# Attention scores from 64-partition halves, in units of four heads by two rows

## The chip, the core and the metric

The kernel runs on one core of one Trainium2 chip. A core has TensorE (in the rows: PE for matmuls, PEld for loads of the stationary operand), VectorE (DVE), ScalarE (ACT), GpSimd (POOL) and SyncE (SP), which here issues nearly all DMAs. The metric is the device time of one execution in microseconds (us), as the median of several runs.

## What is computed

Pooled-key attention, then a top-1 mixture of experts, then a gated layer. The change lies in the first part; the sizes are batch 8, 8 heads, 576 rows, head width 64, all float32:

```python
k_p = k.reshape(B, H, Sp, pool, D).mean(axis=3)      # pool 8: 72 pooled rows
v_p = v.reshape(B, H, Sp, pool, D).mean(axis=3)
scores = scale * np.matmul(q, k_p.transpose(0, 1, 3, 2))
scores = scores - np.max(scores, axis=-1, keepdims=True)
attn = np.exp(scores)
attn = attn / (np.sum(attn, axis=-1, keepdims=True) + 1e-09)
return np.matmul(attn, v_p)
...
x = _moe_ref(x=x, **moe_kwargs)      # expert = argmax of x @ w_gate, 4608 tokens
return _moe2_ref(x=x, **moe2_kwargs)
```

## The kernel before

Attention runs over 36 tiles of 128 tokens. The tiles go in four groups (`m`) of nine: four tiles for each of the batches 2m and 2m+1, and one "mix" tile that holds the last 64 rows of both. A normal tile takes one row r of every group of four token rows, for all 8 heads.

A tile n has these steps on TensorE, each in float32:

- `emit_qt`: q is turned so that the head width lies on partitions. Two heads lie side by side on the 128 partitions. For tiles whose q was loaded as four rows per descriptor (`four_rows`, `two_rows`; 30 of the 32 normal tiles) this is eight matmuls against an identity (L382), each filling 64 of the 128 columns; the others and the mix tiles take four true transposes (L387).
- `emit_sc`: four matmuls (L399), one for each pair of heads, with 128 partitions of q and a block-diagonal `kbd` of 2 x 72 columns whose other half is zero. The mix tile (L402) splits its tokens into two halves of 64 columns.
- `emit_pt` turns the exponentials (L423); `emit_av` multiplies by v (L433 for the first six tiles, L441 and L444 after).

DVE makes the row maximum, the subtraction, the reciprocal, the gate logits `lgs` and the product `x`; ACT evacuates PSUM and makes the exponential; `store` writes `x` to DRAM, one tile at a time, from five buffers.

`kbd` of a batch is made from sums over rows: for batches 2 to 7 `sum_k` (POOL) and `prep_k` (four matmuls L325) give the first 64 pooled rows, and `load_end`, `sum_k(GB)`, `prep_k(GB)` and `end_k` the last 8 of six batches at once (L325 with `se`). Batches 0 and 1 go by `load_rows` on 72 partitions, `sum_rows` and `rows_k` (four transposes L299).

The order of work is written by hand. The main loop over n issues pt(n), exp(n+1), qt(n+3), place "a", sc(n+2), place "b", av(n), store(n-1), places "c", "d", "e"; every engine takes its own instructions in that order. The table `ORDER` puts loads and k/v preparation of later groups at such places (five to a tile; the first number holds for group 1, the second for groups 2 and 3), all loads and stores go through the one SP queue in that order, and `E1` does the same for batch 1. Large loads share a pool of 36 tiles (`wtile`).

Of the kernel before, what the change touches and what calls it, by code (L numbers as in the profile page):

```python
# [36 lines left out]
GB = (2, 3, 4, 5, 6, 7)  # L37
# [12 lines left out]

E1 = [3, 26, 9, 7, 10, 19, 20, 31, 24]
# [8 lines left out]
C_ID, C_IE, C_OFF, C_P, C_PK, C_TRI, C_TOK, C_END = 0, 128, 136, 144, 147, 211, 339, 375  # L60


def constants():
    c = np.zeros((128, C_END), np.float32)
    p = np.arange(128)
    c[:, C_ID:C_ID + 128] = np.eye(128)
    c[:, C_TRI:C_TRI + 128] = p[:, None] < p[None, :]
    c[p, C_PK + p // 2] = 1.0 / 64
    c[:, C_IE:C_IE + E] = np.arange(E)
# [12 lines left out]
def fused(ctx: ExitStack, tc: tile.TileContext, q, k, v, moe_w_gate, moe_w1, moe_w2,  # L82
# [106 lines left out]
    x_p = actx.enter_context(tc.tile_pool(name="xo", bufs=5))  # L189
# [3 lines left out]
    kbd = [at4.tile([128, 4, 2, NP], F32, name=f"kbd{i}") for i in range(3)]  # L193
# [18 lines left out]
    def load_q(b, rs=(0, 1, 2, 3)):  # L212
        t = kq["q", b] if ("q", b) in kq else [wtile(F32, f"q{z}") for z in range(2)]
        for r in rs:
            nc.sync.dma_start(
                out=t[r // 2][:, 512 * (r % 2):512 * (r % 2) + 512].rearrange("p (h d) -> p h d", h=H),
                in_=q[b, :, 0:512, :].rearrange("h (p r) d -> r p h d", r=4)[r])
        kq["q", b] = t

    def load_q2(b, j):  # L220

        t = kq["q", b] if ("q", b) in kq else [wtile(F32, f"q{z}") for z in range(2)]
        nc.sync.dma_start(
            out=t[j].rearrange("p (h n) -> p h n", h=H),
            in_=q[b, :, 0:512, :].rearrange("h (p r) d -> p h (r d)", r=4)[:, :, 128 * j:128 * j + 128])
        kq["q", b] = t
        two_rows.add((b, j))

    two_rows, four_rows = set(), set()

    def load_q4(b, j):

        t = kq.setdefault(("q", b), [])
        x = wtile(F32, f"q{j}")
        nc.sync.dma_start(
            out=x.rearrange("p (h n) -> p h n", h=4),
            in_=q[b, 4 * j:4 * j + 4, 0:512, :].rearrange("h (p r) d -> p h (r d)", r=4))
        t.append(x)
        four_rows.add(b)

    def load_mix(m):
        x = kv1.tile([128, DM], F32, tag="mxq", name="mxq")
# [7 lines left out]
    def load_end(h4):  # L250

        t = kq.setdefault(("k", GB), [])
        t.append(wtile(F32, f"ke{h4}"))
        for h in range(4):
            nc.sync.dma_start(
                out=t[h4][0:16 * len(GB), 256 * h:256 * h + 256],
                in_=k[GB[0]:GB[-1] + 1, 4 * h4 + h, 512:576, :].rearrange("b (p r) d -> b p (r d)", r=4))

    def rows_of(b):
        return 128 if isinstance(b, int) else 16 * len(b)  # L260

    def sum_k(b):
        n = rows_of(b)
        o = kv1.tile([128, DM], F32, tag="sk", name="sk") if n == 128 else wtile(F32, "se")[:, 0:DM]
        for h4 in range(2):
            x = kq["k", b][h4].rearrange("p (h r d) -> p h r d", h=4, r=4)[0:n]
            nc.gpsimd.tensor_tensor(out=x[:, :, 0:2], in0=x[:, :, 0:2], in1=x[:, :, 2:4], op=ALU.add)
            nc.gpsimd.tensor_tensor(
                out=o[0:n, 256 * h4:256 * h4 + 256].rearrange("p (h d) -> p h d", h=4),
                in0=x[:, :, 0], in1=x[:, :, 1], op=ALU.add)  # L270
        kq["k", "sum", b] = o

# [29 lines left out]
    def rows_k(b):  # L302
        pp = turn("k", b)
        for z in range(2):
            nc.scalar.activation(out=kbd[b % 3][64 * z:64 * z + 64, :, z], in_=pp[64 * z:64 * z + 64],
                                 func=AF.Copy, scale=1.0 / 64)
# [12 lines left out]

    def prep_k(b):  # L320
        n = rows_of(b)
        s_ = kq["k", "sum", b]
        pp = ps.tile([128, 4, n // 2], F32, tag="pp", name="pk")
        for hp in range(4):
            nc.tensor.matmul(pp[:, hp], lhsT=s_[0:n, hp * 128:hp * 128 + 128], rhs=cc[0:n, C_PK:C_PK + n // 2])  # L325
        if isinstance(b, int):
            kb = kbd[b % 3]
            nc.scalar.copy(out=kb[0:64, :, 0, 0:64], in_=pp[0:64])
            nc.scalar.copy(out=kb[64:128, :, 1, 0:64], in_=pp[64:128])
        else:  # L330
            kt = kv1.tile([128, 4, n // 2], F32, tag="kt", name="kt")
            nc.scalar.copy(out=kt, in_=pp)
            for j, c in enumerate(b):
                ends[c] = kt, j

    def end_k(b):
        kb = kbd[b % 3]
        kt, j = ends[b]
        for z in range(2):
            zs = slice(64 * z, 64 * z + 64)  # L340
            nc.scalar.copy(out=kb[zs, :, z, 64:NP], in_=kt[zs, :, 8 * j:8 * j + 8])
# [25 lines left out]

    def emit_qt(n):
        m, i = tl[n]
        pq = ps.tile([128, 4, 128], F32, tag="pq", name="pq")  # L370
        for hp in range(4):
            if i < 8:
                b = 2 * m + i // 4
                r = i % 4
                if b in four_rows or (b, r // 2) in two_rows:
                    for z in range(2):
                        h = 2 * hp + z
                        if b in four_rows:
                            src = kq["q", b][h // 4][:, 256 * (h % 4) + 64 * r:256 * (h % 4) + 64 * r + 64]
                        else:  # L380
                            src = kq["q", b][r // 2][:, 128 * h + 64 * (r % 2):128 * h + 64 * (r % 2) + 64]
                        nc.tensor.matmul(pq[64 * z:64 * z + 64, hp], lhsT=src, rhs=ident)  # L382
                    continue
                src = kq["q", b][r // 2][:, 512 * (r % 2) + 128 * hp:512 * (r % 2) + 128 * hp + 128]
# [3 lines left out]
        qt = at_p.tile([128, 4, 128], F32, tag="qt", name="qt")  # L388
        nc.scalar.copy(out=qt, in_=pq)
        qts[n] = qt  # L390

    def emit_sc(n):
# [3 lines left out]
        for hp in range(4):  # L396
            o = sc[:, hp // 2, 144 * (hp % 2):144 * (hp % 2) + 144]
            if i < 8:
                nc.tensor.matmul(o, lhsT=qt[:, hp], rhs=kbd[(2 * m + i // 4) % 3][:, hp])  # L399
            else:  # L400
                for z in range(2):
                    nc.tensor.matmul(o[64 * z:64 * z + 64], lhsT=qt[:, hp, 64 * z:64 * z + 64],  # L402
                                     rhs=kbd[(2 * m + z) % 3][:, hp])
# [24 lines left out]
    def emit_av(n, between=None):  # L428
# [3 lines left out]
        for h in range(H) if n in PLAIN else ():  # L432
            nc.tensor.matmul(av[:, h // 4, 73 * (h % 4):73 * (h % 4) + 73], lhsT=sb[0:NP, h // 4, h % 4],  # L433
                             rhs=vau[(2 * m + i // 4) % 2][:, h])
        for g in range(2) if n not in PLAIN else ():

            for c in range(3):
                kw = dict(start=c == 0, stop=c == 2, skip_group_check=True)
                o = av[:, g, 73 * c:73 * c + 146]
                if i < 8:  # L440
                    nc.tensor.matmul(o, lhsT=sb[:, g, c], rhs=vbd[(2 * m + i // 4) % 3][:, g, c], **kw)  # L441
# [8 lines left out]
        xf = x_p.tile([128, XW], F32, tag="x", name="x")  # L450
        lh = sm_p.tile([128, 2, 4, E], F32, tag="lh", name="lh")
        nc.vector.tensor_tensor(out=lh, in0=a4[:, :, :, D + 1:73], in1=rs.to_broadcast([128, 2, 4, E]), op=ALU.mult)
        nc.vector.tensor_reduce(out=lgs[:, n], in_=lh.rearrange("p a h e -> p e (a h)"), axis=AX.X, op=ALU.add)
# [4 lines left out]
        else:  # L458
            ac = a4[:, :, :, 0:D]
        nc.vector.tensor_tensor(out=xf[:, 0:DM].rearrange("p (a h d) -> p a h d", a=2, h=4), in0=ac,  # L460
                                in1=rs.to_broadcast([128, 2, 4, D]), op=ALU.mult)
        done[n] = xf
# [3 lines left out]
    def store(n):  # L466
        xf = done.pop(n)
        nc.scalar.copy(out=xf[:, DM:XW], in_=lgs[:, n])
        m, i = tl[n]
        if i < 8:  # L470
            b = 2 * m + i // 4
            nc.sync.dma_start(
                out=x_d[b * S:b * S + 512, :].rearrange("(p r) d -> p r d", r=4)[:, i % 4], in_=xf)
        else:
            for z in range(2):
                t0 = (2 * m + z) * S + 512
                nc.sync.dma_start(out=x_d[t0:t0 + 64, :], in_=xf[64 * z:64 * z + 64])

    def route_steps(n0, n1):
# [3 lines left out]
        def r1():  # L483
# [7 lines left out]
            cand = sm1.tile([128, n, E], F32, tag="rcd", name="rcd")  # L491
# [191 lines left out]
    for j in range(2):  # L683
        steps[f"q{j}"] = lambda b, j=j: load_q4(b, j)
# [6 lines left out]
    for i, f, x in ((E1[0], sum_rows, ("k", 1, 3, nc.vector)), (E1[1], place_v, (0,)), (E1[2], rows_k, (1,)),  # L691
                    (E1[3], sum_rows, ("v", 1, 2, nc.vector)), (E1[4], sum_rows, ("v", 1, 3, nc.vector)),
# [702 lines left out]
```

## Time and profile before

| | |
|---|---|
| median of 3 runs | 1649.22 us (1646.08 to 1649.38) |
| the profiled execution, its own time | 1658.23 us |
| its span, first to last instruction | 1656.4 us |
| TensorE matmul busy | 1601.1 us, 97% |
| VectorE busy | 845.0 us, 51% |
| ScalarE busy | 500.4 us, 30% |
| GpSimd busy | 262.0 us, 16% |
| mean granted TensorE clock | 0.986 |

The profiled execution lies 9.0 us above the median of the runs; 1.8 us of its time lie outside the span. Busy shares are means over stages: attention fills about the first 235 us, and in it VectorE and GpSimd are far busier than their share of the span tells. A granted clock of 1.00 is 2.4 GHz, 0.50 is 1.2 GHz.

### The profile page before, as it was taken

What the parts mean: (1) busy time and instruction counts of PE and PEld (TensorE: products, weight loads), DVE (VectorE), ACT (ScalarE), POOL (GpSimd) and SP (SyncE); (2) the same over time, 40 slices, a digit from 0 to 9 for tenths busy, and PEclk for the clock granted to TensorE, in tenths of its full rate; (3) what the DMA queues carried; (4) which work ended last, traced back from release to release, by engine and by line L of the source; (5) the groups of instructions that cost most, each with busy time, mean ns of one, the idle gap of its engine ahead of it and who ended that gap; (6) DMA issues with size and microseconds to landing.
All of it is one profiled execution on the core that took longest, in us unless ns stands there. A gap on an engine that the chain in (4) does not pass through costs nothing. (4 is left out here: it accounts for less than half of the span.)

```text
span 1656.4 us, 26527 instructions
## 1 busy us (share of the span) xinstructions
PE 1601.1 (97%) x9323; PEld 1382.9 (83%) x9323; DVE 845.0 (51%) x1796; ACT 500.4 (30%) x1052; POOL 262.0 (16%) x362
## 2 busy tenths in 40 slices
PE   8999989999999989999999999999999999999997
PEld 6888888888888978998888888888888888888886
DVE  7667686687867687324443433333443333443222
ACT  3544543455434354322212212121211212122121
POOL 5766472101110111103000000000000000000000
PEclk9989999999999999999999999999999999999999
DMA  7967776376845563217400100010010001000000
GB/s 199 275 144 190 166 111 199 103 250 230 274 154 195 177 217 131 70 52 259 119 13 20 32 13 26 13 39 13 14 34 15 29 13 33 20 1 26 0 26 13
DMA packets 125371, 161.95 MB, mean 98 GB/s; under 512 B 38544, under 2 KB 83728, under 8 KB 125216
## 3 DMA queue, kind: packets, MB, share of 16 engines
q1 hardware_dynamic: 113440, 124.13, 27.0%
q0 software_dynamic: 11776, 35.91, 6.9%
q8 instruction: 78, 1.28, 0.3%
q14 instruction: 77, 0.63, 0.2%
HBM read 116.92 MB, written 43.08 MB: 97 GB/s over the span
## 5 line engine op out<-in xcount | busy, mean ns | idle before, releaser
L1292 DVE SCALAR_TENSOR_TENSOR th<-th,g 128x512 f32<-128x512 f32 (+1 forms) x120 | 76.1, 634 | 470.6 <-ACT th L1291 470.6
L1288 PE MATMUL g<-xl,rh 128*128 128x512 f32 (+1 forms) x576 | 217.3, 377 | 0.0
L1289 PE MATMUL g<-xh,rl 128*128 128x512 f32 (+1 forms) x576 | 217.3, 377 | 0.0
L1287 PE MATMUL g<-xh,rh 128*128 128x512 f32 (+1 forms) x576 | 217.3, 377 | 0.0
L1291 ACT ACTIVATE th<-g 128x512 f32<-128x512 f32 (+1 forms) x120 | 66.6, 555 | 460.6 <-PE g L1289 460.6
L1318 POOL DMA_INDIRECT out_dram<-o,tk x36 | 34.6, 962 | 815.8 <-ACT o L1317 785.4
L1313 PE MATMUL po<-rl,a 128*128 128x512 f32 x360 | 140.3, 390 | 1.6 <-DMA rl<-scr 1.6
L1312 PE MATMUL po<-rh,a 128*128 128x512 f32 x360 | 140.2, 390 | 0.0
L1314 PE MATMUL po<-rh,a 128*128 128x512 f32 x360 | 140.0, 389 | 0.0
L1287 PEld LDWEIGHTS g<-xh,rh 128*128 128x128 f32 x576 | 108.4, 188 | 20.3
L1288 PEld LDWEIGHTS g<-xl,rh 128*128 128x128 f32 x576 | 108.4, 188 | 20.2
L1289 PEld LDWEIGHTS g<-xh,rl 128*128 128x128 f32 x576 | 108.4, 188 | 19.9
L545 PE MATMUL p<-xh,w1h 128*128 128x256 f32 x672 | 110.2, 286 | 11.2 <-DVE hl L548 8.8
L146 ACT CAST a<-th 128x512 fp32r<-128x512 f32 (+1 forms) x120 | 69.3, 578 | 167.2 <-DVE th L1293 167.2
L147 DVE TENSOR_TENSOR a<-th,a 128x512 fp32r<-128x512 f32 (+1 forms) x120 | 76.7, 639 | 77.2 <-ACT a L146 77.2
L1287 PE MATMUL g<-xh,uh 128*128 128x512 f32 (+1 forms) x288 | 108.7, 378 | 1.7 <-DVE th L1293 1.7
L1288 PE MATMUL g<-xl,uh 128*128 128x512 f32 (+1 forms) x288 | 108.6, 377 | 0.0
L1289 PE MATMUL g<-xh,ul 128*128 128x512 f32 (+1 forms) x288 | 108.6, 377 | 0.0
L545 PE MATMUL p<-xh,w1l 128*128 128x256 f32 x672 | 108.0, 283 | 0.0
L545 PEld LDWEIGHTS p<-xh,w1h 128*128 128x128 f32 x672 | 94.3, 193 | 16.1 <-DVE hl L548 9.6
L545 PE MATMUL p<-xl,w1h 128*128 128x256 f32 x672 | 107.7, 283 | 0.0
L548 DVE SCALAR_TENSOR_TENSOR hl<-p,hh 128x256 fp32r<-128x256 f32 x168 | 70.6, 421 | 64.5 <-ACT hh L547 57.3
(283 smaller groups left out, 3025.5 us busy)
## 6 DMA issues: line engine op xcount, KB each, us to landing
st<-in_moe_w_dram SPq DMA_DIRECT2D x64, 512.0 KB
y_d<-ys SPq DMA_DIRECT2D x39, 257.0 KB
v<-in_v_dram SPq DMA_DIRECT2D x32, 288.0 KB
y<-y_d SPq DMA_DIRECT2D x68, 128.0 KB
x_d<-x SPq DMA_DIRECT2D x32, 260.0 KB
q<-in_q_dram SPq DMA_DIRECT2D x15, 512.0 KB
scr<-uh SPq DMA_DIRECT2D x13, 512.0 KB
scr<-ul SPq DMA_DIRECT2D x13, 512.0 KB
```

The lines of the kernel that those rows point to most:

```text
L146: nc.scalar.copy(out=hi, in_=src)
L147: eng.tensor_tensor(out=lo, in0=src, in1=hi, op=ALU.subtract)
L545: nc.tensor.matmul(a, lhsT=w[d][:, fs], rhs=x[:, d], start=j + d == 0, stop=j == 2 and d == 3)
L548: nc.vector.scalar_tensor_tensor(out=lo, in0=a, scalar=0.0, in1=hi, op0=ALU.max, op1=ALU.subtract)
L1287: nc.tensor.matmul(g[:, j], lhsT=wh[:, sl], rhs=hi[:, d], start=d == 0, stop=False)
L1288: nc.tensor.matmul(g[:, j], lhsT=wh[:, sl], rhs=lo[:, d], start=False, stop=False)
L1289: nc.tensor.matmul(g[:, j], lhsT=wl[:, sl], rhs=hi[:, d], start=False, stop=d == 3)
L1291: nc.scalar.activation(out=th, in_=g[:, 0], func=AF.Tanh, scale=0.5)
L1292: nc.vector.scalar_tensor_tensor(out=th, in0=th, scalar=1.0, in1=g[:, 0], op0=ALU.add, op1=ALU.mult)
L1312: nc.tensor.matmul(po, lhsT=a[:, 0, tsl], rhs=wh[:, sl], start=c == 0, stop=False)
L1313: nc.tensor.matmul(po, lhsT=a[:, 0, tsl], rhs=wl[:, sl], start=False, stop=False)
L1314: nc.tensor.matmul(po, lhsT=a[:, 1, tsl], rhs=wh[:, sl], start=False, stop=c == NC2 - 1)
```

## The change

A normal tile becomes a unit of four heads (g = i % 2) and two rows (2j and 2j+1 of every four). Two rows of one head lie next to each other in the load, so q is turned by four true transposes for every unit, with row 2j on partitions 0 to 63 and row 2j+1 on 64 to 127. The scores are then eight matmuls of 64 partitions by 72 columns, alternating between the lower and the upper half, into two PSUM banks. For that, `kbd` holds every head on both halves: `prep_k` takes seven products of 128 columns and two of 64, and `end_k` takes two products for each batch out of row sums of the ends (`load_ends`, `sum_ends`) in three groups of batches, 0, 1 to 3 and 4 to 7. The mix tile uses q padded with zeros and sixteen products in place of eight. Batches 0 and 1 use the same path as the rest. Two units share an `x` tile and are stored after the second; there are three such tiles. The gate logits of two units are reduced together. The load of batch 3's second q half, and the first loads, move.

```diff
-GB = (2, 3, 4, 5, 6, 7)
+EB = ((0,), (1, 2, 3), (4, 5, 6, 7))
...
-    ("q00", 6, 11), ("q10", 15, 18), ("q01", 25, 28), ("q11", 36, 36)]
+    ("q00", 6, 11), ("q10", 15, 18), ("q01", 20, 28), ("q11", 24, 36)]
...
-    x_p = actx.enter_context(tc.tile_pool(name="xo", bufs=5))
+    x_p = actx.enter_context(tc.tile_pool(name="xo", bufs=3))
...
-    kbd = [at4.tile([128, 4, 2, NP], F32, name=f"kbd{i}") for i in range(3)]
+    kbd = [at4.tile([128, H, NP], F32, name=f"kbd{i}") for i in range(3)]
...
+    def load_q(b, g, j=None):
+        t = kq["q", b] if ("q", b) in kq else kq.setdefault(("q", b), {})
+        if g not in t:
+            t[g] = wtile(F32, f"q{g}")
+        c = slice(0, 256) if j is None else slice(128 * j, 128 * j + 128)
         nc.sync.dma_start(
+            out=t[g].rearrange("p (h n) -> p h n", h=4)[:, :, c],
+            in_=q[b, 4 * g:4 * g + 4, 0:512, :].rearrange("h (p r) d -> p h (r d)", r=4)[:, :, c])
...
+    def load_ends(bs, eng=None):
+        x = wtile(F32, "ke")
+        n = len(bs)
+        for h in range(H):
+            (eng or nc.sync).dma_start(
+                out=x[16 * h:16 * h + 16, 0:256 * n].rearrange("p (b n) -> p b n", b=n),
+                in_=k[bs[0]:bs[-1] + 1, h, 512:576, :].rearrange("b (p r) d -> p b (r d)", r=4))
...
+    def both_k(b):
+        return kbd[b % 3].rearrange("p (h o) s -> p o h s", o=2)
+    def of_k(b, h, z):
+        return kbd[b % 3][64 * z:64 * z + 64, (h - z) % 8]
...
-        for hp in range(4):
-            nc.tensor.matmul(pp[:, hp], lhsT=s_[0:n, hp * 128:hp * 128 + 128], rhs=cc[0:n, C_PK:C_PK + n // 2])
+        pp = ps.tile([128, 2, 4, 64], F32, tag="pp", name="pk")
+        for c in range(8):
+            o = pp[:, c % 2, c // 2]
+            if c < 7:
+                nc.tensor.matmul(o, lhsT=s_[:, 64 * c:64 * c + 128], rhs=PK)
+            else:
+                for z in range(2):
+                    h = (7 + z) % 8
+                    nc.tensor.matmul(o[64 * z:64 * z + 64], lhsT=s_[:, 64 * h:64 * h + 64], rhs=PK)
+        nc.scalar.copy(out=both_k(b)[:, :, :, 0:64], in_=pp)
     def end_k(b):
+        pp = ps.tile([128, H, 8], F32, tag="pp", name="pe_")
         for z in range(2):
+            nc.tensor.matmul(pp[64 * z:64 * z + 64], lhsT=ends[b], rhs=cc[:, C_PK + 8 * z:C_PK + 8 * z + 64])
+        nc.scalar.copy(out=kbd[b % 3][:, :, 64:NP], in_=pp)
...
             if i < 8:
-                        nc.tensor.matmul(pq[64 * z:64 * z + 64, hp], lhsT=src, rhs=ident)
+                j, g = i % 4 // 2, i % 2
+                src = kq["q", 2 * m + i // 4][g][:, 256 * hp + 128 * j:256 * hp + 128 * j + 128]
...
             nc.tensor.transpose(pq[:, hp], src, ident)
...
-                nc.tensor.matmul(o, lhsT=qt[:, hp], rhs=kbd[(2 * m + i // 4) % 3][:, hp])
+        if i < 8:
+            for h in range(4):
                 for z in range(2):
+                    nc.tensor.matmul(sc[:, z, NP * h:NP * h + NP], lhsT=qt[64 * z:64 * z + 64, h],
+                                     rhs=of_k(2 * m + i // 4, 4 * (i % 2) + h, z))
+        else:
+            for h in range(H):
+                for y in range(2):
+                    ys_ = slice(64 * y, 64 * y + 64)
+                    nc.tensor.matmul(sc[ys_, h // 4, NP * (h % 4):NP * (h % 4) + NP],
+                                     lhsT=qt[:, h % 2, h // 2, ys_], rhs=kbd[(2 * m + y) % 3][:, h - h % 2])
...
-    keep_warm(28)
-    load_rows(k, 0, "k")
+    keep_warm(24)
+    load_k(0)
     nc.sync.dma_start(out=cc, in_=cst[:, 0:C_TRI])
-    load_q(0, (0,))
+    load_q(0, 0, 0)
+    load_ends(EB[0], nc.scalar)
     load_rows(v, 0, "v")
...
-    load_q(0, (1,))
-    load_q2(0, 1)
-    load_rows(k, 1, "k")
-    load_q4(1, 0)
-    load_q4(1, 1)
+    load_q(0, 1, 0)
+    load_q(0, 0, 1)
+    load_k(1)
+    load_q(0, 1, 1)
+    load_ends(EB[1])
+    load_q(1, 0)
     load_rows(v, 1, "v")
+    load_q(1, 1)
```

How the instructions stand now, at three places. On PE, a normal tile of group 0 into group 1; `pt` is the turned exponentials, `pq` the turned q, `pvg` a part of v's preparation, `sc` the scores. Before:

```order
L423 MATMUL pt<-cc,pe 96x128 x6
L382 MATMUL pq<-cc,q_453 64x128 x4
L382 MATMUL pq<-cc,q_569 64x128 x4
L347 MATMUL pvg<-wg,vt 72x16 x4
L399 MATMUL sc<-kbd_130,qt 128x144 x4
L441 MATMUL av<-vbd_132,ptsb 128x146 x6
```

and now:

```order
L417 MATMUL pt<-cc,pe 96x128 x6
L372 MATMUL pq<-cc,q_560 128x128 x4
L335 MATMUL pvg<-wg,vt 72x16 x4
L390 MATMUL sc<-kbd_130,qt 128x72 x8
L435 MATMUL av<-vbd_132,ptsb 128x146 x6
```

A unit reads one q tile and not two, its q takes four instructions and not eight, and its scores eight of half the columns.

On PE again, where batch 2's keys are made (`pk`, at tile 4). Before:

```order
L433 MATMUL av<-vau_134,ptsb 128x73 x8
L325 MATMUL pk<-cc,sk 128x64 x4
L325 MATMUL pk<-cc,se 128x48 x4
L423 MATMUL pt<-cc,pe 72x128 x8
L387 MATMUL pq<-cc,mxq 128x128 x4
```

and now:

```order
L427 MATMUL av<-vau_134,ptsb 128x73 x8
L318 MATMUL pk<-cc,sk 128x64 x7
L322 MATMUL pk<-cc,sk 64x64 x2
L417 MATMUL pt<-cc,pe 72x128 x8
L372 MATMUL pq<-cc,mxq 128x128 x4
```

The products of the keys are seven and two in place of four, and the four on the ends of six batches are gone.

On SP, the loads ahead of batch 3 (`q_732` and `q_927` before, `q_639` and `q_699` now, are batch 3's two q halves; `k_728`, `k_730`, now `k_722`, `k_724`, its keys; `k_812` and `v_850` on are batch 4's). Before:

```order
L206 DMA k_728<-in_k_dram 128x4x256
L206 DMA k_730<-in_k_dram 128x4x256
L235 DMA q_732<-in_q_dram 128x4x256
L472 DMA x_d<-x 128x520
L206 DMA k_812<-in_k_dram 128x4x256
L206 DMA k_814<-in_k_dram 128x4x256
L472 DMA x_d<-x 128x520
L278 DMA v_850<-in_v_dram 72x2x512
L278 DMA v_852<-in_v_dram 72x2x512
L278 DMA v_854<-in_v_dram 72x2x512
L278 DMA v_856<-in_v_dram 72x2x512
L235 DMA q_927<-in_q_dram 128x4x256
```

and now:

```order
L216 DMA q_639<-in_q_dram 128x4x256
L481 DMA x_d<-x 128x520 x2
L216 DMA q_699<-in_q_dram 128x4x256
L205 DMA k_722<-in_k_dram 128x4x256
L205 DMA k_724<-in_k_dram 128x4x256
L205 DMA k_808<-in_k_dram 128x4x256
L205 DMA k_810<-in_k_dram 128x4x256
```

Both q halves of batch 3 now stand ahead of its keys, and ahead of batch 4's keys and values.

## Rows read from the trace of the kernel before

**Rows 1.** Windows: stretch, length; busy us (instructions) by engine; granted clock, DMA share, GB/s.

```profile
29.60:85.90 56.30, 51.40 (x513) 47.07 (x513) 39.11 (x84) 28.54 (x70) 41.43 (x52) 1.00 0.90 240
85.90:100.00 14.10, 14.10 (x76) 13.16 (x77) 5.26 (x9) 4.05 (x9) 5.65 (x8) 0.53 0.86 173
100.00:235.00 135.00, 126.44 (x1207) 115.89 (x1206) 103.95 (x274) 70.54 (x177) 87.75 (x117) 0.97 0.68 156
```

**Rows 2.** Timeline of PE: start, length, line, out<-in, [idle before]. Two tiles.

```profile
208.75 0.82 PE L423 MATMUL pt<-cc,pe 128*96 128x128 f32 x6
209.50 1.09 PE L382 MATMUL pq<-cc,q 128*64 128x128 f32 x16
210.52 1.25 PE L399 MATMUL sc<-kbd,qt 128*128 128x144 f32 x8
211.61 1.66 PE L441 MATMUL av<-vbd,ptsb 96*128 96x146 f32 x12
213.11 0.82 PE L423 MATMUL pt<-cc,pe 128*96 128x128 f32 x6
213.76 0.60 PE L387 MATMUL pq<-cc,mxq 128*128 128x128 f32 x4
214.20 1.15 PE L399 MATMUL sc<-kbd,qt 128*128 128x144 f32 x8
```

**Rows 3.** Timeline, a mix tile's product with v, in two column halves.

```profile
131.25 0.13 PEld L444 LDWEIGHTS av<-both,ptsb 96*64 96x64 f32 x1
131.25 0.34 PE L444 MATMUL av<-both,ptsb 96*64 96x146 f32 x1
131.25 0.13 PEld L444 LDWEIGHTS av<-vbd,ptsb 96*64 96x64 f32 x1
131.25 0.34 PE L444 MATMUL av<-vbd,ptsb 96*64 96x146 f32 x1
...
131.42 0.29 PE L444 MATMUL av<-both,ptsb 96*64 96x146 f32 x1
...
131.55 0.29 PE L444 MATMUL av<-both,ptsb 96*64 96x146 f32 x1
```

**Rows 4.** Timeline of PE, products of few moving columns behind full stationary loads.

```profile
31.29 1.90 PE L433 MATMUL av<-vau,ptsb 72*128 72x73 f32 x16
33.03 0.42 PE L299 MATMUL ptk<-cc,sk 72*128 72x72 f32 x4
...
50.97 1.09 PE L325 MATMUL pk<-cc,se 96*128 96x48 f32 x8 [0.83 <-ACT kbd L329]
```

**Rows 5.** Timeline of PE, batch 4's keys, and the product after them.

```profile
148.22 1.00 PE L325 MATMUL pk<-cc,sk 128*128 128x64 f32 x8
149.06 1.71 PE L441 MATMUL av<-vbd,ptsb 96*128 96x146 f32 x12
```

**Rows 6.** Timeline of PE, the waits for loads of q.

```profile
22.50 1.09 PE L382 MATMUL pq<-cc,q 128*64 128x128 f32 x16
...
29.62 0.66 PE L382 MATMUL pq<-cc,q 128*64 128x128 f32 x8 [1.41 <-DMA q<-in_q_dram]
...
34.25 1.09 PE L382 MATMUL pq<-cc,q 128*64 128x128 f32 x16
...
85.88 0.66 PE L382 MATMUL pq<-cc,q 128*64 128x128 f32 x8 [3.03 <-DMA q<-in_q_dram]
...
140.62 0.66 PE L382 MATMUL pq<-cc,q 128*64 128x128 f32 x8 [1.12 <-DMA q<-in_q_dram]
```

**Rows 7.** Timeline of SP, the issue of batch 3's second q half.

```profile
69.19 0.39 SPq L235 DMA_DIRECT2D q<-in_q_dram  x1
```

**Rows 8.** Windows, columns as in Rows 1: the front, and a stretch of group 2.

```profile
0.00:29.62 29.62, 24.31 (x165) 15.34 (x166) 20.38 (x23) 9.34 (x17) 14.42 (x28) 1.00 0.85 220
121.00:138.00 17.00, 16.73 (x176) 15.21 (x175) 13.38 (x33) 8.35 (x22) 13.19 (x20) 1.00 1.01 251
```

More of the change, by code (lines that the diff above doesn't have):

```diff
@@ L248, in load_mix @@
         kq["q", "mix", m] = x
[L250 to L260, printed above, removed]
+    def load_ends(bs, eng=None):
[5 more added lines that the diff above has]
+                in_=k[bs[0]:bs[-1] + 1, h, 512:576, :].rearrange("b (p r) d -> p b (r d)", r=4))
+        kq["ke", bs] = x
@@ new lines, in add_four, with sum_ends @@
+    def add_four(o, x, eng):
+        if eng is nc.vector:
+            eng.tensor_reduce(out=o, in_=x.rearrange("p h r d -> p h d r"), axis=AX.X, op=ALU.add)
+            return
+        eng.tensor_tensor(out=x[:, :, 0:2], in0=x[:, :, 0:2], in1=x[:, :, 2:4], op=ALU.add)
+        eng.tensor_tensor(out=o, in0=x[:, :, 0], in1=x[:, :, 1], op=ALU.add)
+    def sum_ends(bs, eng=None):
+        n = len(bs)
+        o = kv1.tile([128, 256], F32, tag="es", name="es") if n > 1 else kv1.tile([128, D], F32, tag="es0", name="es0")
+        add_four(o[:, 0:64 * n].rearrange("p (b d) -> p b d", b=n),
+                 kq["ke", bs][:, 0:256 * n].rearrange("p (b r d) -> p b r d", b=n, r=4), eng or nc.gpsimd)
+        for j, b in enumerate(bs):
+            ends[b] = o[:, 64 * j:64 * j + 64]
@@ L262, in sum_k, with sum_half @@
+    def sum_half(b, h4, eng=None):
+        if ("k", "sum", b) not in kq:
+            kq["k", "sum", b] = kv1.tile([128, DM], F32, tag="sk", name="sk")
+        add_four(kq["k", "sum", b][:, 256 * h4:256 * h4 + 256].rearrange("p (h d) -> p h d", h=4),
+                 kq["k", b][h4].rearrange("p (h r d) -> p h r d", h=4, r=4), eng or nc.gpsimd)
     def sum_k(b):
-        n = rows_of(b)
-        o = kv1.tile([128, DM], F32, tag="sk", name="sk") if n == 128 else wtile(F32, "se")[:, 0:DM]
         for h4 in range(2):
[L266 to L270, printed above, removed]
@@ L271, in sum_k @@
-        kq["k", "sum", b] = o
+            sum_half(b, h4)
     def load_rows(src, b, nm, hs=(0, 1, 2, 3)):
@@ L366, in fused, with zeros @@
     qts, scs, pes, pts = {}, {}, {}, {}
+    qzs = {}
+    def zeros(m):
+        qzs[m] = wtile(F32, "qz").rearrange("p (z h t) -> p z h t", z=2, h=4)
+        for z in range(2):
+            nc.gpsimd.memset(qzs[m][64 * (1 - z):64 * (1 - z) + 64, z], 0.0)
     def emit_qt(n):
@@ L757, in fused @@
     nc.gpsimd.memset(run_c, 0.0)
-    for h in range(4):
-        sum_rows("k", 0, h, nc.gpsimd if h == 2 else nc.vector)
-    rows_k(0)
+    sum_half(0, 0, nc.vector)
+    sum_half(0, 1)
+    sum_ends(EB[0], nc.vector)
     emit_qt(0)
+    prep_k(0)
+    end_k(0)
     sum_rows("v", 0, 0, nc.vector)
     sum_rows("v", 0, 1, nc.gpsimd)
-    keep_warm(3)
     emit_sc(0)
     emit_exp(0)
-    keep_warm(9)
+    keep_warm(6)
     sum_rows("v", 0, 2, nc.vector)
```

147 lines of the change are left out of this document (53 added, 94 removed).

## The prediction, made before the changed kernel ran

> **What bounds the kernel now.** I read the page first: TensorE matmuls fill 97% of the span. A mean says nothing of attention, so next come the windows [rows 1]. From 29.6 to 85.9 us TensorE is busy in 51.40 of 56.30 us, from 100 to 235 us in 126.44 of 135; between them lie 14.10 us in which it is busy all the time at a clock of 0.53. So attention is bound by TensorE nearly everywhere, and what its instructions save or add there is the first thing to count; what it waits for is the second. No other engine is full on average in these windows (VectorE has 39.11 and 103.95 us, GpSimd 41.43 and 87.75).
>
> The timeline of TensorE tells what a tile costs. A tile whose q goes through the identity matmuls starts at 208.75 and its successor at 213.11: 4.36 us, made of 0.75 for `pt`, 1.02 for q, 1.09 for the scores, 1.50 for the product with v, taken from start to start. In the tile after it q is turned by four true transposes: `pt` takes 0.65 and q 0.44, and the scores' record is 1.15 instead of 1.25 [rows 2]. The 0.10 at each of the two borders is what going from full-width products to 64-column ones and back costs there.
>
> The waits of TensorE that matter are for loads of q: 1.41 us at 29.62, 3.03 at 85.88, 1.12 at 140.62 [rows 6]. The second is the dear one, since the clock stood at about a half for the 14.10 us that follow: at full clock the same work would take 14.10 x 0.53 = 7.5 us, so 6.6 us went there on top of the 3.0. The load waited for was issued at 69.19 [rows 7], 16.7 us before its wait ended: it stood at the back of a full queue.
>
> **The change, part by part.** I sum on TensorE, for what counts on the path, and then turn to waits.
>
> *Turning q.* Thirty tiles go from identity matmuls to transposes. By the two tiles in [rows 2] one gains 0.10 + 0.58 + 0.10 = 0.78 us. Three of them (the third to fifth) lie in the front, where TensorE waits for loads anyway. 27 x 0.78 = **21 us gained**.
>
> *The scores.* Eight products of 64 partitions by 72 columns take the place of four of 128 by 144. A float32 product is two passes, so 16 passes. No row shows a product of 64 partitions, so I bound it. Where few columns move behind a load of 128 stationary columns, the load sets the pace: 16 passes of 73 columns take 33.03 - 31.29 = 1.74 us, 0.109 each [rows 4]. If lower and upper half run one behind the other, the scores take 16 x 0.109 = 1.74 us. If they run side by side, half of that, 0.87. The nearest row for two parts of the array at work together is the mix tile, where the two column halves start in pairs at the same 131.25, loads and products, with 0.13 us from pair to pair [rows 3]: both halves did a full pace's work at once. I take side by side, as the alternation of halves and the separate banks are the same there. The borders of 0.10 come back, now around the scores. Against the 0.98 without borders that is +0.1 us a tile, 30 x 0.1 = **3 us lost**; one behind the other it is 1.74 + 0.2 - 0.98 = +0.96 a tile, 29 us lost.
>
> The Trainium skill (TensorE: Matmul & The Clock Gate, Part 3, "The mechanism") says that a stationary load overlaps products in flight only when their row groups differ. The 0.109 us a pass in [rows 4] speaks against the "only": there each load hid behind the product before it within the full array. By the rule the halves would overlap and the sum be that of side by side; by the row alone both stay possible.
>
> *The keys.* `prep_k` was 8 passes in 149.06 - 148.22 = 0.84 us [rows 5]; now it is 14 passes at 0.109, two pairs at 0.13 [rows 3] and two borders, 1.53 + 0.26 + 0.2 = 2.0 us. For batches 2 to 7 that is 6 x 1.16 = 7.0 us more. Batch 1 paid four transposes, at most 0.42 [rows 4]: 1.6 more. Batch 0 lies in the front. `end_k` is two pairs and two borders, some 0.4 us, for seven batches 2.8. The block on the ends of six batches goes, 0.9 us of work and 0.83 of waiting for its PSUM tile [rows 4]: 1.7 back. **Net 9.7 us lost.** At tile 6 the ends of batches 3 and 2 and v's transposes follow each other through one PSUM tile, each waiting for ScalarE: about **1 us**, once (0 to 2).
>
> *The mix tiles* double their score products at half the columns. In column halves the row of 0.13 a pair for 146 columns [rows 3] covers 72 columns at half of that, so nothing changes; if the 64-column loads set the pace instead, it is 0.5 us a tile. I take 0.
>
> *The waits for q.* A unit needs one q half, so the first tile of batch 3 no longer needs the second; and that half now goes out ahead of batch 3's keys and batch 4's keys and values, 3.2 MB by their shapes. At the 240 GB/s of the window [rows 1] that is some 13 us earlier. So 3.0 + 6.6 at 85.88 go, and 1.1 at 140.62, where the half waited for is needed one tile later: **10.7 us gained**. What is late next is batch 3's keys, 1.0 MB later in the queue, 4 us: I expect their sums at about 74 us, when TensorE comes for them. Then batch 4's values at about 83 us; TensorE reaches that place at 83 to 84.
>
> *The front.* By 29.62 us the core moved 220 GB/s x 29.62 = 6.5 MB [rows 8]. The fourth tile's q now stands behind batch 1's keys, 4.6 MB of loads; with the 0.8 MB that were in flight beyond the loads landed, that is 24.5 us, where TensorE asked at 22.50 [rows 6]. The fifth then is no longer late (1.4 us back), and the sixth stands behind 7.2 MB, at about 35.4 us, where TensorE asked at 34.25. **1 us lost** (-2 to +3). ScalarE's eight early load issues come before it has any work.
>
> *VectorE and the rest.* In a stretch of group 2 VectorE is busy 13.38 of 17 us in 33 instructions [rows 8]; with small gaps between them little is free if TensorE's part of this stretch shrinks by some 1.7 us. I charge **3 us** over attention (0 to 7, the most that the work from 100 us on can give). Stores of pairs, fewer and larger copies of keys and logits, and the zeros for mix tiles lie on ScalarE, with 70.54 us busy of 135, and GpSimd [rows 1]: nothing while those have room. If `x` stores land late, three paired tiles hold as long as five single ones within a tile.
>
> Sum: -21 + 3 + 9.7 + 1 - 10.7 + 1 + 3 = **-14 us**. The profiled execution took 1658.2, so it would be 1644; it lies 9.0 us above the median of the runs, 1649.2, from which the same difference gives **1635 us**. After attention the program is as it was, and TensorE's work there shifts as a whole.
>
> **The rivals.**
> 1. *The halves run one behind the other.* Place: each unit's scores. The sum has 29 in place of 3, and the 3 of VectorE fall away since nothing there is squeezed: -14 + 26 - 3 = +9, **1658 us**, slower. It decides from the point where a unit's scores cost 0.6 us more than I take (30 x 0.6 against 14 + 3). For it: the pace of 0.109 a pass is shown, the overlap of 64-partition halves is not. Against: the pairs of [rows 3].
> 2. *The wait for q is replaced by one for batch 3's keys or batch 4's values*, of about 3 us, and the clock falls again as it did after 85.88: 9.6 of the gain come back, -14 + 9.6 = -4, **1645 us**. For it: the queue is busy at 0.90 in that window [rows 1], and the margins above are below 1 us. Against: batch 3's keys need not be whole before the first products start.
> 3. *The clock.* The share of TensorE's time in transposes goes from 0.65 of 4.36 us a tile to 1.09 of 3.7. If the clock falls to its half level for the stretch of a batch or two, a tile costs up to 3.7 us more; four tiles eat the gain, six give +8, **1657 us**. Against: the tile at 213.11 has 1.09 us of transposes and keeps its pace [rows 2], and 100 to 235 us show 0.97 [rows 1]. The Trainium skill speaks for it (TensorE: Matmul & The Clock Gate, Part 4): it says that transposes don't count as work for the clock in the way that products do. One tile at full pace doesn't settle that.
>
> **How the numbers follow.** The forecast gets 0.55, rival 2 gets 0.20, rival 1 gets 0.15, rival 3 gets 0.10. A measurement of this kernel can tell about 0.2%, 3.3 us, from no change. Faster by more: 0.54 of the forecast, 0.12 of rival 2, 0.02 of each other rival: 0.70. Slower: 0.11 of rival 1, 0.06 of rival 3, 0.02 of rival 2: 0.19. Within: 0.11. The forecast's own range, from its bounds (front 3 either way, VectorE 0 to 7, mix and tile 6 together 3), is 1627 to 1643. To leave no more than 2 in 10 out, the range takes in rival 2 and the near part of rivals 1 and 3: **1626 to 1652**.
>
> **What the profile after would show.** Right: the scores of a unit in about 1.0 us, with starts in pairs; q in 0.45 us; `pk` in about 2 us; a unit without k or v work in some 3.7 us; no wait for q near 80 us, and the clock near 1.00 from 30 to 100 us. Wrong: scores of 1.7 us or more (rival 1); a wait of TensorE of 3 us or more in the keys of batch 3 or behind VectorE's sum of batch 4's values, with a clock near 0.5 after it (rival 2); a clock below 1.00 where TensorE doesn't wait (rival 3). The end of attention, where the last `pt` starts, should lie 10 to 18 us earlier; if it does and the whole time doesn't follow, the handing over to the experts was bound by something else.

## The result and the profile after

The changed kernel is slower: a median of 1662.54 us over 22 runs, beside 1647.17 us over 22 runs of the kernel before on the same chip, ratio 1.0082 [1.0060, 1.0103], some 13.5 us. On a second chip the ratio was 1.0069 [1.0031, 1.0106] (`e12_after` below). The forecast was 14 us faster, range 1626 to 1652. A run over 1.5% above the fastest of its kernel is left out of every mean below.

The profiled execution took 1665.4 us (span 1663.6, mean clock 0.981; before 1656.4 and 0.986). Its windows, to be read against [rows 1, 8] (columns as there: stretch, length; busy us by engine; granted clock, DMA share, GB/s):

```profile
0.00:29.62 29.62, 26.23 (x184) 17.80 (x185) 14.37 (x19) 9.10 (x18) 11.71 (x23) 0.88 0.83 210
29.60:85.90 56.30, 52.21 (x478) 47.89 (x477) 34.85 (x68) 23.43 (x54) 34.97 (x46) 0.88 0.98 242
85.90:100.00 14.10, 14.10 (x143) 13.03 (x142) 12.16 (x22) 8.03 (x19) 12.37 (x16) 1.00 0.76 191
100.00:235.00 135.00, 122.83 (x1223) 113.58 (x1222) 102.63 (x256) 67.16 (x156) 89.27 (x119) 0.94 0.86 152
```

The half clock behind 85.88 is gone (1.00 where [rows 1] has 0.53), and so is the wait for q there. In its place the clock is 0.88 in the two stretches ahead, where before it was 1.00.

The work itself came out near the forecast, with one term too small. TensorE's timeline, first the keys of a batch, then a unit:

```profile
124.33 1.67 PE L318 MATMUL pk<-cc,sk 128*128 128x64 f32 x14
125.93 0.34 PE L322 MATMUL pk<-cc,sk 128*64 128x64 f32 x4
126.19 0.86 PE L417 MATMUL pt<-cc,pe 128*96 128x128 f32 x6
```

```profile
101.22 0.84 PE L417 MATMUL pt<-cc,pe 128*96 128x128 f32 x6
101.90 0.60 PE L372 MATMUL pq<-cc,q 128*128 128x128 f32 x4
102.43 1.12 PE L390 MATMUL sc<-kbd,qt 64*128 64x72 f32 x16
103.48 1.76 PE L435 MATMUL av<-both,ptsb 96*128 96x146 f32 x12
105.08 0.41 PE L289 MATMUL ptv<-cc,sv 72*128 72x72 f32 x4
```

From start to start the keys take 1.86 us (2.0 forecast), q 0.53, the scores 1.05, the product with v 1.60, the unit 3.86 where the tile at 208.75 in [rows 2] took 4.36. In [rows 2] q by transposes took 0.44 and the product with v 1.50, so the two borders around the scores, 0.09 and 0.10, lie outside their 1.05: with borders they take 1.24, and 1.08 was forecast. A unit gains 0.50 us, where 0.78 - 0.10 = 0.68 was forecast, some 5 us less over 30 units. And attention ends no earlier: the last `pt` starts at 227.96 us, in two profiles of before at 224.99 and 228.64, and the last ranks' product at 238.40, before at 237.11. What fell out as work came back as half clock and waits.

A number for that can be had from every run, not only from a profile, since each lists its mean granted clock: time x (1 - clock) is what the run lost to the clock, time x clock the rest, called kept below. This takes all time at half clock for work, and the clock is listed to 0.001, which is 1.7 us in one run. The changed kernel's 22 runs lose 32.9 us on average and keep 1628.0. On the second chip, 11 runs of it lose 34.9 and keep 1630.6; 29 runs of the kernel before lose 19.5 and keep 1633.2. So the change makes the rest 2.6 us shorter and loses 15.4 us more to the clock (standard errors 1.0 and 2.5). The experiments look for both numbers: why only 2.6, and what takes the 15.

### The profile page after: what moved, and what is told of

Its sections match the earlier page's. It is cut to its first block, busy times and chain, and to the rows that moved or that the text cites. A ratio compares the mean times of both kernels' runs of the same rounds, so it can differ in the third digit from the quotient of the medians.

```text
span 1663.6 us, 26628 instructions
## 1 busy us (share of the span) xinstructions
PE 1602.1 (96%) x9384; PEld 1384.0 (83%) x9385; DVE 841.4 (51%) x1777; ACT 497.0 (30%) x1027; POOL 264.4 (16%) x363
```

## Experiments

### First round: the places where the trace waits

The theory then was that single waits bring the half clock: the lost q wait of before, the chain of ends at tile 6 (waits of 0.50, 0.31 and 0.28 us at 66.66 to 67.87, half clock until 78), and a wait of 1.33 us for the ends of batch 0 at 12.57. The rival was that the loss is spread over the units.

`e1_before` is the kernel before, unchanged.

> The kernel before once more, unchanged, to see what its typical execution looks like. The theory that the profiled execution was typical expects a wait of TensorE of about 3 us for batch 3's second q half near 86 us, with a clock near 0.5 behind it, and a mean clock of 0.986 in most runs. The rival, that this wait and the clock loss behind it (9.6 us) belonged to that one execution, which lay 9 us above the median, expects no such wait or a shorter one, a mean clock of 0.990 or more in most runs, and time times clock of some 1635 us in all.

Measured: ratio 0.9984 [0.9956, 1.0012]; 21.5 us lost to the clock, mean clocks 0.983 to 0.989. The wait for q came again, 4.7 us long, with less half clock behind it (below): neither theory holds whole.

`e2_q_order`: before, with the change's places for q alone.

```diff
-    ("q00", 6, 11), ("q10", 15, 18), ("q01", 25, 28), ("q11", 36, 36)]
+    ("q00", 6, 11), ("q10", 15, 18), ("q01", 20, 28), ("q11", 24, 36)]
```

> The kernel before with only batch 3's two q loads moved up in the load order, as the change does. If the 9.6 us of the forecast were there to be had in a typical execution, this gives 5 to 10 us. If they belonged to one execution, it gives between 2 us gained and 2 us lost.

Measured: 0.9995 [0.9966, 1.0025]. TensorE's waits for q from 30 to 290 us, by line and releaser (us in total, times, longest), in e1 and then in e2:

```profile
PE pq L382 <- DMA q<-in_q_dram: 8.5, 2, 4.7
```

```profile
PE pq L382 <- DMA q<-in_q_dram: 1.1, 1, 1.1
```

7.4 us of waits go and the time stays (medians 1655.80 and 1656.22), although in the two profiles the last `pt` of e2 starts 8.0 us earlier. In the stretch 85.90 to 100 us e1's clock was 0.89, not 0.53: a wait of 4.7 us was followed by a loss of 14.10 x 0.11 = 1.6 us, and the 6.6 us of [rows 1] were one execution's.

`e3_ends_apart`: the changed kernel with the ends of the two batches at tile 6 apart.

```diff
-    ("kend0", 34, 29)   ("kend1", 33, 43)
+    ("kend0", 30, 29)   ("kend1", 38, 43)
```

> The changed kernel, with the ends of batches 2 and 3 (end_k) each at a place of its own instead of one behind the other at tile 6. Theory: in the changed kernel the clock falls behind short waits, and the waits there, 1.5 us in all, cost them and about 5 us of clock behind them; then this gives 4 to 7 us against the changed kernel, about 1.004 against the kernel before. Rival: the loss is spread over all tiles, because the new instructions hold the clock less well; then it gives under 2 us, about 1.008.

Measured: 1.0086 [1.0053, 1.0120], as the changed kernel.

`e4_front`: the changed kernel with one q load ahead of batch 1's values, and warm products (matmuls whose result nobody reads) around the ends of batch 0.

```diff
+    keep_warm(6)
     end_k(0)
+    keep_warm(1)
...
-    keep_warm(6)
+    keep_warm(9)
```

> The changed kernel with its front changed: batch 1's second q half is loaded ahead of batch 1's values, and warming matmuls fill TensorE's waits before the first scores (six and one more there, nine instead of six behind them). The theory that the front costs its waits and the clock behind them (3.6 us of clock before 29.6 us, 1.5 us of wait at 36 us and about 2 us of clock behind it) expects 4 to 7 us gained against the changed kernel, about 1.004 against the kernel before. The rival that the loss is spread over all tiles expects under 2 us.

Measured: 1.0101 [1.0051, 1.0151]. The clock of the first 29.62 us was 1.00 again, but from 29.60 to 85.90 it was 0.88 as in the changed kernel. Mending single waits gained nothing: the first theory fell.

### Second round: stores in pairs

The share of busy DMA engines from 100 to 235 us is 0.86 at 152 GB/s, against 0.68 at 156 in [rows 1]. The two rows of a pair are stored together.

`e5_one_store`: the changed kernel, one store for both rows.

```diff
-            for z in range(2):
-                nc.sync.dma_start(out=rows[:, 2 * j + z], in_=xf[:, z])
+            nc.sync.dma_start(out=rows[:, 2 * j:2 * j + 2], in_=xf)
```

> The changed kernel with the two stores of a pair of rows as one: 128 pieces of 4160 bytes in place of 2 x 128 of 2080. Theory T3 (the pair of stores, issued together, holds the transfer engines: DMA share 0.86 at 152 GB/s in 100 to 235 us against 0.68 at 156 GB/s before, and the first expert's weights land at 252.7 us against about 246): DMA share of 100 to 235 us under 0.78, no wait for row_i at the hand-over, ratio 0.992 to 1.003. Theory T2 (the new matmuls hold TensorE's clock less well, whatever the transfers do): ratio 1.005 to 1.010 even if the DMA share falls.

Measured: 1.0063 [1.0037, 1.0090], DMA share 0.88. Neither time nor share fell clearly.

`e6_before_pairs`: before, with an even tile's store held back to the odd tile's.

```diff
     def store(n):
+        i = tl[n][1]
+        if i < 8 and i % 2 == 0:
+            return
+        for c in (n - 1, n) if i < 8 else (n,):
+            store_one(c)
```

> The kernel before with one edit: the store of an even tile waits for that of the odd tile behind it, so that both are issued together, as the changed kernel does. T3: DMA share of 100 to 235 us rises from about 0.70 to 0.80 or more, the first expert's weights come late, ratio 1.004 to 1.010. T2: ratio 0.998 to 1.003, since no TensorE instruction changes.

Measured: 1.0073 [1.0050, 1.0095]; of the mean difference of 11.1 us 4.8 are clock (24.6 lost, 19.8 in before's runs beside it) and 6.3 are not (1638.05 kept, 1631.75). The DMA share rose as expected, 0.85 in the stretch:

```profile
100.00:235.00 135.00, 118.98 (x1139) 109.27 (x1137) 102.06 (x269) 67.65 (x170) 88.02 (x116) 0.96 0.85 158
```

So pairs cost the kernel before something by themselves. Where they do, this profile doesn't tell: the execution took 1655.1 us, well under its median of 1664.5.

`e7_stores_apart`: the changed kernel, the second store one unit later in the program.

```diff
-            for z in range(2):
-                nc.sync.dma_start(out=rows[:, 2 * j + z], in_=xf[:, z])
+            nc.sync.dma_start(out=rows[:, 2 * j], in_=xf[:, 0])
+            second[n + 1] = rows[:, 2 * j + 1], xf[:, 1]
```

> The changed kernel with the second store of a pair one unit (about 4 us) later than the first. T3, if it is the coming together: DMA share of 100 to 235 us near 0.70, ratio 0.994 to 1.003. T3, if it is something else in the stores: DMA share stays over 0.82 and ratio 1.006 to 1.010. T2: 1.005 to 1.010 whatever the DMA share.

Measured: 1.0153 [1.0128, 1.0178], a miss, with a DMA share of 0.83 from 100 to 235 us. SP issues the second store 0.4 us behind the first in six of the 16 pairs and 1.0 to 8.4 us behind it in the others, so the stores are apart only in part; and VectorE now waits for an `x` tile to come free:

```profile
DVE x L466 <- DMA x_d<-x: 7.6, 2, 6.6
```

`e8_act_stores` and `e9_before_act` issue the stores of `x` from ScalarE, in the changed kernel and in before.

```diff
-                nc.sync.dma_start(out=rows[:, 2 * j + z], in_=xf[:, z])
+                nc.scalar.dma_start(out=rows[:, 2 * j + z], in_=xf[:, z])
```

> The changed kernel with its stores of x issued by ScalarE, on a queue of their own, so that no load stands behind a pair of stores. T3 (what is lost is lost by loads that stand behind pairs of stores on one queue): the first expert's gate weights land before 249 us, the wait of 2 to 3 us for row_i goes, ratio 0.999 to 1.004. T2 (the new TensorE work holds the clock less well): granted clock of 29.6 to 85.9 us stays at 0.76 to 0.88, ratio 1.005 to 1.010.

> The kernel before with its stores of x issued by ScalarE. Control to the run before: T3 expects little, since stores come one by one there (0.997 to 1.003); T2 the same. Over 1.004: the queue of its own costs something by itself, and the run before must be read against this one.

Measured: 1.0156 [1.0117, 1.0194] and 1.0119 [1.0084, 1.0153]. The queue of its own costs before 19 us, so the pair of runs says little about pairs of stores. It does bear on the clock: the changed kernel loses 12.1 us more to it here than before does (41.9, 29.8) and keeps 6.2 us less, with the stores of `x` on another queue than the loads. And e9, with no product on half rows, loses 10.5 us more than before does beside it (19.3): this measure rises for other reasons as well.

### Third round: the handing over to the experts

In the changed kernel the last stores stand ahead of the first expert's weights. The timeline there: ScalarE and VectorE wait for the gate weights (`us`), and TensorE then for VectorE's `row_i`:

```profile
235.14 0.80 SPq L481 DMA_DIRECT2D x_d<-x  x2
236.34 3.37 SPq L486 DMA_DIRECT2D x_d<-x  x2
239.82 0.61 SPq L938 DMA_DIRECT2D us<-in_moe_w_gate_dram  x1
...
252.66 0.67 ACT L957 ACTIVATE ub<-us 128x512 f32<-128x512 f32 x1 [6.21 <-DMA us<-in_moe_w_gate_dram]
252.67 0.43 DVE L960 TENSOR_SCALAR ua<-us 128x512 int32<-128x512 int32 x1 [3.75 <-DMA us<-in_moe_w_gate_dram]
...
257.07 0.66 PE L585 MATMUL px<-cc,both 128*128 128x128 f32 x4 [2.03 <-DVE row_i L904]
```

Before, the load was issued at 236.07 and ScalarE had it at 245.98. Four runs on one chip: e12_after is the changed kernel as it is, e13_last_pair moves one store, e14_front_last is that with e4's front, e15_pairs_last moves the same store in e6. The edit of the store:

```diff
+        if n == NTL - 1:
+            store(n - 1)
         if n < NTL - 1:
             emit_av(n)
...
-        if n:
+        if 0 < n < NTL - 1:
             store(n - 1)
```

> The changed kernel as it is, beside the three that follow. Its ratio is the one they are to be read against: 1.006 to 1.010. Its stretch from the last count of the tokens (cn) to the transpose of og should be 30 us or more again, against 26 to 29 in five profiles of before.

> The changed kernel with one step moved: ScalarE copies the logits of the last pair ahead of its copy of the last tile's values, not behind it. In four profiles of the changed family that pair is ready at about 230 us, its store issues at 235, and stores of 533 + 266 KB then lie ahead of the first expert's weights. Hand-over theory: the store issues about 5 us earlier, the gate weights land 10 us behind their issue and not 13, DVE does not wait 4 to 6 us for them, cn to og's transpose falls from 30 to 32 us to under 28; 4 to 6 us less than e12_after, ratio 1.002 to 1.006. If the loss is spread over the tiles alone (T2): same as e12_after within 2 us.

> e13_last_pair with the front of e4_front (three more warm products ahead of the ends of batch 0, one behind, one q load ahead of values; the clock of the first 29.6 us was 1.00 there against 0.88, and the first ranks came at 64.8 us against 67 to 77 in six others of the changed family and 62.8 to 67.4 in before). If both places count: 2 to 4 us less than e13_last_pair, ratio 0.999 to 1.004. If e4's front did not matter: as e13_last_pair.

> e6_before_pairs (the kernel before, stores in pairs, 1.0073) with the same step moved as in e13_last_pair. If what pairs cost the kernel before is also a late last pair: ratio 1.000 to 1.004. If pairs cost all along the tiles: 1.005 to 1.010.

Measured: e12_after 1.0069 [1.0031, 1.0106], e13_last_pair 1.0102 [1.0065, 1.0138], e14_front_last 1.0092 [1.0056, 1.0129], e15_pairs_last 1.0074 [1.0046, 1.0101]. In the profiles of e13 and e14 the stretch from the last count to og's transpose is 27.7 and 27.8 us, as expected; but it was 26.4 in e12_after, where the last pair happened to go out early, and in e13 the gate weights still came 13.3 us behind their issue (241.58 to 254.91). No time was won in either kernel. Late weights are seen in most profiles of the changed family, but in e2 as well (231.68 to 245.43), and e12_after took 1674.95 us in its profile with that stretch short. So they are not needed for the changed kernel to be slower; what they cost was not isolated. Read against each other, e13 and e15, which both store in pairs, differ by 7.2 us kept (1631.5, 1638.7) and 12.6 us of clock the other way (38.0, 25.4 lost).

### Fourth round: the clock

From 29.60 to 85.90 us the clock is 0.61 to 0.88 in all the profiles of the changed kernel and its variants (e18 below is the lowest), and 0.97 to 1.00 in those of before, but for 0.88 in e9_before_act behind a wait of 4.2 us. In e3 and e5 it falls at 50 us and no wait over 0.31 us stands in the 6 us ahead of that. Now the theory, called T2 in the expectations, was: the score products on 64 partitions hold the clock less well than those on 128.

`e10_fill` and `e18_fill_more` add products on full rows to the changed kernel, six a unit in tiles 2 to 15, or fourteen in tiles 2 to 12; `e11_before_fill` adds the six to before.

```diff
+        for z in range(6) if 2 <= n < 16 else ():
+            nc.tensor.matmul(sc[:, z % 2, 288:416], lhsT=ones, rhs=ones)
```

> The changed kernel with six bf16 products of 128 x 128 by 128 x 128 behind the scores of tiles 2 to 15, into columns that nobody reads: about 0.06 us each at full clock, 5 us in all if nothing hides them. T2 (in 29.6 to 85.9 us the changed kernel's clock is 0.76 to 0.88 in five profiles and 0.97 to 1.00 in four of before, and falls at 50 us behind no wait over 0.31 us): clock of that stretch 0.97 or more, ratio 1.000 to 1.006, under the changed kernel's 1.0082. T3: clock unchanged or changed with no gain, ratio 1.009 to 1.013.

> The kernel before with the same six products in the same tiles. T2 and T3: no clock to be won there, so it pays what the products cost, 1 to 5 us, ratio 1.000 to 1.004.

> The changed kernel with fourteen bf16 products of 128 x 128 by 128 x 128 (e10_fill had six, and clocks 0.79 in 29.6 to 85.9 us) behind the scores of tiles 2 to 12: some 0.85 us of full rows a unit, 9 us if nothing hides them. T2: clock of 29.6 to 85.9 us 0.95 or more, ratio 1.001 to 1.006. If full rows do not hold the clock: clock under 0.90 and ratio 1.011 to 1.016.

Measured: e10 1.0078 [1.0048, 1.0107], clock 0.79 in the stretch; e11 1.0020 [0.9993, 1.0047]; e18 1.0113 [1.0072, 1.0154], clock 0.61. In these profiles filling doesn't hold the clock up, against what was expected. The means over runs leave it open: e10 loses 9.6 us more to the clock than before does beside it and e18 11.0, where the changed kernel loses 15.4, with standard errors of 2.8, 4.6 and 2.5 and on other chips.

`e16_before_half` puts the half-row products, and nothing else of the change, into the kernel before; `e17_before_whole` is its control. So that the two halves can go to two banks, a pair is now head h and head h + 4 (q is turned head by head, the sums of k lie in that order, and the mix tile's scores take 32 passes); e17 has these too.

```diff
-                nc.tensor.matmul(o, lhsT=qt[:, hp], rhs=kbd[(2 * m + i // 4) % 3][:, hp])
+                for z in range(2):
+                    zs = slice(64 * z, 64 * z + 64)
+                    nc.tensor.matmul(sc[:, z, NP * hp:NP * hp + NP], lhsT=qt[zs, hp], rhs=kb[zs, z])
```

In e17 the last line is

```diff
+                    nc.tensor.matmul(sc[:, z, NP * hp:NP * hp + NP], lhsT=qt[:, hp], rhs=kb[:, z])
```

> The kernel before with the scores of its whole tiles in the changed kernel's form: per head pair two products over 64 partitions each, in two PSUM banks, in place of one over 128 partitions by 144 columns (the heads of a pair are h and h + 4 for that; q is turned head by head in the few tiles where it was not, the mix tile's scores take 32 passes). T2 (the half-row products hold TensorE's clock less well): granted clock of 29.6 to 85.9 us falls from 0.97 to 1.00 to 0.90 or less, without a longer wait ahead of the fall, clock lost over the run rises from 20 to 28 us or more, ratio 1.004 to 1.010. If it is the stores, keys or loads of the change and not the scores: clock of that stretch 0.96 or more, ratio 0.998 to 1.003.

> The control to e16_before_half: the same products, order and banks, but each over all 128 partitions (the other half of the stationary block meets zeros in k), one behind the other: some 0.7 us more for each of 32 tiles, 22 us if nothing hides them. T2: clock of 29.6 to 85.9 us 0.96 or more, ratio 1.008 to 1.016 from the work alone. If the order and banks of the products let the clock fall and not the half rows: clock there 0.90 or less as well.

Measured, beside 11 runs of before that lose 20.1 us to the clock and keep 1631.5:

| | ratio | clocks of its runs | lost to the clock | kept |
|---|---|---|---|---|
| before | | 0.986 to 0.991 | 20.1 us | 1631.5 us |
| e16, half rows | 1.0124 [1.0094, 1.0154] | 0.977 to 0.983 (6) | 33.2 us | 1638.8 us |
| e17, whole rows | 1.0140 [1.0105, 1.0175] | 0.986 to 0.990 (5) | 21.5 us | 1655.6 us |

The control pays for its longer products, 24 us, and loses 1.4 us more clock than before, within the noise. With the half rows the kernel keeps 7 us more than before and loses 13 more to the clock, nearly what the whole change loses. No run of e16 has a clock that a run of e17 or of before has.

The timeline of e16, TensorE, and the windows around it, show a fall with no wait over 0.36 us in the 17 us ahead of it:

```profile
39.89 1.98 PE L434 MATMUL av<-vau,ptsb 72*128 72x73 f32 x16 [0.36 <-DVE x L461]
41.71 0.42 PE L301 MATMUL ptv<-cc,sv 72*128 72x72 f32 x4
41.96 1.04 PE L424 MATMUL pt<-cc,pe 128*72 128x128 f32 x8
42.93 1.09 PE L385 MATMUL pq<-cc,q 128*64 128x128 f32 x16
43.95 0.69 PE L349 MATMUL pvg<-wg,vt 128*72 128x16 f32 x8
44.57 1.11 PE L399 MATMUL sc<-kbd,qt 64*128 64x72 f32 x16
45.62 2.30 PE L434 MATMUL av<-vau,ptsb 72*128 72x73 f32 x16
47.72 1.90 PE L327 MATMUL pk<-cc,sk 128*128 128x64 f32 x8
```

```profile
29.60:47.00 17.40, 17.04 (x196) 15.66 (x197) 13.77 (x26) 8.49 (x20) 11.20 (x15) 1.00 0.85 247
47.00:67.00 20.00, 19.17 (x110) 17.55 (x111) 7.92 (x19) 6.05 (x13) 9.21 (x11) 0.50 0.86 280
67.00:85.90 18.90, 18.17 (x215) 16.36 (x212) 11.61 (x28) 8.86 (x24) 11.23 (x15) 0.98 0.69 192
```

TensorE is busy in 17.04 of 17.40 us, the clock falls, and it stays at half for 20 us although TensorE is busy in 19.17 of them; the eight `pk` passes take 1.90 us where they take 1.00 in [rows 5]. One profile alone would not settle it: the profiled execution of e17 has such a stretch as well, from 54 to 75 us, there at a wait of 0.83 us,

```profile
54.49 1.77 PE L327 MATMUL pk<-cc,se 96*128 96x48 f32 x8 [0.83 <-ACT kbd L331]
```

```profile
54.00:75.00 21.00, 20.51 (x131) 19.06 (x132) 7.13 (x15) 6.34 (x14) 6.57 (x8) 0.52 0.68 202
75.00:85.90 10.90, 10.18 (x96) 9.36 (x97) 6.75 (x17) 5.04 (x15) 5.48 (x7) 0.99 0.58 161
```

so that its clock from 29.60 to 85.90 is 0.82, as in e16, and 56.30 x 0.18 = 10.1 us are lost there in both. This is what was expected of e17 if order and banks, and not the half rows, let the clock fall. The two part only later, first e16, then e17:

```profile
100.00:235.00 135.00, 126.97 (x1416) 115.65 (x1412) 103.54 (x254) 69.73 (x172) 81.34 (x108) 0.96 0.78 161
```

```profile
100.00:235.00 135.00, 133.52 (x1380) 124.28 (x1375) 98.16 (x249) 65.97 (x165) 76.97 (x104) 1.00 0.72 160
```

The control's longer products leave TensorE idle for 1.48 of these 135 us, those of e16 for 8.03. So e17 differs from e16 in its gaps as well as in its rows, and it may lose as little as before only because it hardly waits. The means over runs show that the new form of the scores costs clock. That it is the half rows in it, and not two banks or smaller products at this pace, they make likely; a control at e16's pace was not run.

## Why the prediction was wrong

- **Turning q, keys, side-by-side halves: right.** The row above gives 1.05 us for the scores of a unit, 16 passes at 0.066 each where [rows 4] has 0.109; rival 1, one half behind the other, is out. The Trainium skill (TensorE: Matmul & The Clock Gate, "Why this matters for your kernels") says that small products on distinct row groups run at the same time. The trace agrees, with these 16 passes in 1.05 us.
- **The step that failed first is the scores' term.** I gave them 3 us as work and nothing as clock. The work was mis-sized: with borders the scores take 1.24 us and not 1.08, so 30 units lose 8 us and not 3. The clock is 13.1 us in e16, beside the 15.4 that the change loses more than before. Rival 3 had the clock, with a chance of 0.10, but for another reason, the share of true transposes: e16 turns every q by identity products and loses nearly as much. The tile at 213.11 in [rows 2], which was put against rival 3, was no evidence on this: its score products fill 128 rows.
- **The waits for q, 10.7 us, were not there to be gained.** The 6.6 us of half clock were one execution's; e1 waits for q again and loses 1.6 us behind it. e2 takes the waits away and the time doesn't move. In the mean over runs the kernel before loses 20 us to the clock anyway, wherever the waits fall.
- **Stores of pairs: "nothing while those have room".** They were put beside ScalarE's and GpSimd's room, and the queue was not costed. e6 measures 11 us in the kernel before, 6.3 of them outside the clock, and e15 again 5.5.
- **The sum.** Without its clock term the forecast was -14 + 6.6 = -7.4 us; measured is -2.6 outside the clock. Two things are seen that could fill this gap of 4.8: the borders, some 5 us, and the pairs, 5.5 to 6.3. Together they are more than the gap, and e13 beside e15, with pairs in both, keeps 7.2 us less, near the 7.4 of the forecast, as if the borders cost nothing; so the gap is not divided between them here. The clock's term was -6.6 and became +15.4, a miss of 22.0. The gap and this miss are the 26.8 us between -14 and the second chip's +12.8.
- **The front, tile 6, the mix tiles.** The wait for batch 0's ends at 12.57 and the half clock behind it were not in the front's term (1 us); e4 mends them and gains nothing. Tile 6 has its 1.1 us of waits. The mix tile's scores take 1.15 us (60.91 to 62.06), in before 1.07 (59.10 to 60.17), near the 0 taken. One sum in the front does not come out of its terms: 7.2 MB and the 0.8 in flight at 220 GB/s are 36.4 us and not 35.4; the wait there, 1.51 us, ended at 36.15.

Shown: scores in the new form, put into the kernel before, make it lose about 13 us more to the clock, and stores in pairs by themselves cost it about 11. Not settled: whether the half rows in that form do it (e17); whether the two add up in the changed kernel (their clock is 13 + 5 us, its own 15.4 in e12 and 18.5 in e13); by what the pairs cost, since neither one large store nor an earlier last pair took it away and another queue has a cost of its own; and whether added products on full rows hold the clock. No version tried beats the kernel before.

## What to carry to other kernels

Products on half the rows that run side by side saved less of TensorE's time here than their own length says, since a border of about 0.10 us lies on each side of them; count from the start of the product before to the start of the one behind. And such a change can cost by what the clock does over whole runs: put the new form of product alone into the old kernel, next to a control that keeps the pace, and compare mean clocks over runs. A stretch of half clock behind a wait in one profile is not a gain that lies there; only when most executions have it can it be taken back. Stores that come half as often and two at a time cost something in the kernel before, by a way that was not found: cost them and test them alone.

## What the runs showed of the hardware

The clock can fall to half with TensorE busy in 17.04 of 17.40 us and no wait over 0.36 us, and stay there for 20 us, 19.17 of them busy (e16). The same wait can leave it up or be followed by half clock: in before 0.83 us at 50.97 [rows 4] left it at 1.00, and in e2, where `pt` takes 1.61 us and in before 1.04, the clock from 50 to 54 us was 0.57:

```profile
49.21 1.09 PE L325 MATMUL pk<-cc,se 96*128 96x48 f32 x8 [0.83 <-ACT kbd L329]
50.14 1.61 PE L423 MATMUL pt<-cc,pe 128*72 128x128 f32 x8
```

Two score products on the lower and the upper 64 partitions run side by side: 16 passes in 1.05 us. Going from products on full rows to them and back costs 0.09 and 0.10 us (the unit at 101.22 beside [rows 2]).
